# A fused attention and feed-forward kernel: later batches project q and k in plain float32 on TensorE's row halves instead of as split float32r

## The chip, the cores and the metric

The kernel runs on one core of one Trainium2 chip. The metric is the device time of the whole program in microseconds. Before the change it took 1100.27 us (median of three runs, 1098.75 to 1100.88).

## What is computed

Random-feature attention over 8 batches of 8 heads (576 tokens, 64 columns a head, 128 features), then a feed-forward layer over the 4608 tokens (512 to 2048 to 512, exact gelu). All of it is float32.

```
q_s, k_s = q * scale, k * scale            # scale = 64 ** -0.25
phi(x): proj = einsum('bhsd,md->bhsm', x, omega)
        h = proj - sum(x * x, -1) / 2
        h = h - max(h, -1)
        return exp(h) / sqrt(m)
q_p, k_p = phi(q_s), phi(k_s)
kv  = einsum('bhsm,bhsd->bhmd', k_p, v);   z = sum(k_p, axis=2)
num = einsum('bhsm,bhmd->bhsd', q_p, kv)
den = einsum('bhsm,bhm->bhs', q_p, z)[..., None] + 1e-06
x   = (num / den), heads side by side, one row a token
out = gelu(x @ w_in) @ w_out
```

Since the row maximum is taken off, the sum of squares falls out, and the kernel doesn't compute it.

## The kernel before

The attention works on units of two heads of one batch: 32 units, four a batch. The first batch (mode 0) runs before the feed-forward starts, the second (mode 1) and the other six (mode 2, 24 units) run between its matmuls. The feed-forward goes over 12 blocks of 384 tokens and, in each, over 16 chunks of 128 hidden columns. For a chunk, `mm1` (L622) makes twelve matmuls of 384 columns: each product is three, of high and low float32r parts. `act_high` and `act_low` (L629, L630, L635) make the gelu and its two parts, on ScalarE and VectorE. `mm2` (L645 to L647) adds three times three matmuls of 512 columns into three accumulators. The sets of weights are converted into high and low parts in the first fifth of the program, on ScalarE, VectorE and GpSimd (L124 to L155).

The order is written by hand. Every step is an event with a time, in units of which a chunk has 6 and a mode-2 unit 35; the events are issued in the order of their times, and the layer below may then move single instructions. What one engine is given stands in its queue in order, so an instruction that waits holds up all behind it on that engine. PSUM has three pools of banks: `at` (three buffers, all of the attention), `h` (two) and `acc` (three). A buffer of `at` is taken again when its readers are done.

In modes 0 and 1, q and k of the two heads lie on the two halves of the partitions, columns of a head on 64 rows (`x2`). `proj_pair` (L533) then makes four tiles of 128 tokens for each head, in plain float32, with the heads alternating on TensorE's upper and lower row halves. `proj_shared` (L544) makes the tile in which the end of one head meets the start of the other. `proj_mid` (L594, L596) takes the row maximum from PSUM and subtracts it into `et`, the tile of all exponents. The plain numerators (`num`, L459) use column halves.

In mode 2 both halves of the partitions hold the same q and k of both heads (two DMAs each, L223). `x_high` (L236, ScalarE) rounds a piece to float32r on all 128 rows, and `x_low` (L242, GpSimd) replaces its lower half by what the rounding lost, so that one matmul multiplies both parts. For k, five groups: `proj` (L249) multiplies by the high and low part of omega side by side, `proj_lo` (L254, ScalarE) copies the second product, `proj_add` (L260, L261, VectorE) adds it and takes the maximum, and `k_shift` (L266, GpSimd) subtracts that for all nine tiles. For q, four groups: `proj_q` (L277) makes two matmuls of 288 tokens, features on the partitions; `q_blocks` (L285, L287, VectorE) transposes blocks of 32 and takes their maxima; `q_max` (L293) to `q_max4` (L306) find the maximum of a token by two small transposes on TensorE; and `q_shift` (L312, VectorE) subtracts it. Then one exponential over `et` (`exps`, L320).

What follows is shared by both versions: k's exponents as two float16 parts (`k_high`, `k_low`), v in bfloat16 parts (`v_a` to `v_d`, GpSimd), their product in one `at` buffer (`kv`, L400), its copies (`kv_a` to `kv_d`: L409 on ScalarE, L416 to L418 on VectorE, L424, L428), and three float32r matmuls a head for the numerators (L468), whose quotients (`den`, `div`) become the rows x.

SyncE's queue issues the DMAs in order: weights, q, k, v, outputs.

Of the kernel before, what the change touches and what calls it, by code (L numbers as in the profile page):

```python
# [19 lines left out]
P = 128  # L20
# [8 lines left out]
def favor_attention_ffn(ctx: ExitStack, tc: tile.TileContext, qT, kT, v, omT, w_in, w_out, out):  # L29
# [28 lines left out]
    ident = cp.tile([P, P], F32, name="ident")  # L58
    om = cp.tile([P, 2, M], F32R, name="om")
    om32 = cp.tile([P, M], F32, name="om32")  # L60
# [3 lines left out]
    wol = cp.tile([P, NF, DM], F32R, name="wol")  # L64
    xt = cp.tile([P, 2, 2, S], F32, name="xt")
    xf = xt.rearrange("p a h s -> p (a h s)")
    x2 = xt[:, :, 0]
# [27 lines left out]
    def has(u, *ks):  # L95
        assert all(own[k] is u for k in ks), (u.b, u.j, ks)
# [108 lines left out]
    def v_ones(u):  # L205
        nc.vector.memset(u.v[:, :, D:D + 1], 1.0)
        nc.vector.memset(u.v[D:P, MID, D:D + 1], 0.0)
        nc.vector.memset(u.v[0:D, MID + 1, D:D + 1], 0.0)

    def load_x(u):  # L210
        own['x'] = u
# [5 lines left out]
        for s, src in ((1, qT), (0, kT)):  # L217
            if u.mode == 1:
                nc.sync.dma_start(x2[:, s], src[u.b, 2 * u.j:2 * u.j + 2].rearrange("h d s -> (h d) s"))
                continue  # L220
            sv = src[u.b, 2 * u.j:2 * u.j + 2].rearrange("h d s -> d h s")
            for r in range(2):
                nc.sync.dma_start(xt[r * D:(r + 1) * D, s], sv)  # L223
        nc.sync.dma_start(u.v[:, :, 0:D], v[u.b, u.j])


    XG = [(g * P, min(g + 2, NT) * P) for g in range(0, NT, 2)]
    NK = len(XG)
    XG += [(R2 + g * HS, R2 + (g + 1) * HS) for g in range(4)]
    QB = HS // 32  # L230

    def x_high(u, i):
        has(u, 'x')
        a, b = XG[i]
        u.r[i] = p2().tile([P, HS], F32R, tag="r", name="r", bufs=3)
        nc.scalar.copy(u.r[i][:, 0:b - a], xf[:, a:b])  # L236

    def x_low(u, i):
        has(u, 'x')
        a, b = XG[i]  # L240
        r = u.r[i][D:, 0:b - a]
        nc.gpsimd.tensor_tensor(r, xf[D:, a:b], r, op=ALU.subtract)  # L242

    def proj(u, i):
        ps = ps_at()
        r = u.r.pop(i)
        u.pp[i] = ps.rearrange("p (t a m) -> p t a m", t=2, a=2)
        for t in range((XG[i][1] - XG[i][0]) // P):
            nc.tensor.matmul(u.pp[i][:, t], r[:, t * P:(t + 1) * P], om, start=True, stop=True)  # L249

    def proj_lo(u, i):
        n = (XG[i][1] - XG[i][0]) // P
        u.lo[i] = p2().tile([P, 2, M], F32, tag="lo", name="lo", bufs=2)
        nc.scalar.copy(u.lo[i][:, 0:n], u.pp[i][:, 0:n, 1])  # L254

    def proj_add(u, i):
        t0, t1 = XG[i][0] // P, XG[i][1] // P
        own.update({('e', t): u for t in range(t0, t1)})
        es = et[:, t0:t1]
        nc.vector.tensor_tensor(es, u.pp.pop(i)[:, 0:t1 - t0, 0], u.lo.pop(i)[:, 0:t1 - t0], op=ALU.add)  # L260
        nc.vector.tensor_reduce(u.nm[:, t0:t1], es, axis=AX.X, op=ALU.max, negate=True)  # L261

    def k_shift(u):
        has(u, *[('e', t) for t in range(NT)])
        es = et[:, 0:NT]
        nc.gpsimd.tensor_tensor(es, es, u.nm[:, 0:NT].unsqueeze(2).broadcast_to([P, NT, M]), op=ALU.add)  # L266
        done.add((u, 'k'))

# [3 lines left out]

    def proj_q(u, g):
        ps = ps_at()
        r = u.r.pop(NK + g)
        for i in range(2):
            nc.tensor.matmul(ps[:, 0:HS], om[:, i], r, start=(i == 0), stop=(i == 1))  # L277
        u.pp[NK + g] = ps

    def q_blocks(u, g):  # L280
        own['q', g] = u
        if g == 0:
            u.mx = sp.tile([P, 4 * QB], F32, tag="mx", name="mx", bufs=1)
            u.nq = sp.tile([P, 4 * QB], F32, tag="nq", name="nq", bufs=1)
        nc.vector.transpose(ef[:, slice(*XG[NK + g])], u.pp.pop(NK + g)[:, 0:HS])  # L285
# [23 lines left out]
    def q_shift(u):  # L309
        need((u, 'nq'))  # L310
        has(u, *[('q', g) for g in range(4)])
        nc.vector.tensor_tensor(eq, eq, u.nq.unsqueeze(2).broadcast_to([P, 4 * QB, 32]), op=ALU.add)  # L312
        done.add((u, 'q'))

    def exps(u):
        if u.mode == 2:
            need((u, 'k'), (u, 'q'))
        has(u, *[('e', t) for t in range(NT)])
        has(u, *([('e', t) for t in range(NT, 2 * NT)] if u.mode == 1 else [('q', g) for g in range(4)]))
        nc.scalar.activation(et, et, AF.Exp)  # L320
        done.add((u, 'e'))

    def q_back(u, g):
        need((u, 'e'))
        has(u, ('q', g))
        u.qt[g] = p2().tile([P, HS], F32, tag="qt", name="qt", bufs=2)
        nc.vector.transpose(u.qt[g], ef[:, slice(*XG[NK + g])])  # L327

# [183 lines left out]

    def split_om():
        nc.vector.tensor_copy(om[:, 0], om32)
        nc.vector.tensor_tensor(om[:, 1], om32, om[:, 0], op=ALU.subtract)

    def load_plain(u):
        own['x'] = u
        u.nm = sp.tile([P, 2 * NT], F32, tag="nm", name="nm", bufs=2)
        for s, src in ((0, kT), (1, qT)):  # L520
            nc.sync.dma_start(x2[:, s], src[u.b, 2 * u.j:2 * u.j + 2].rearrange("h d s -> (h d) s"))
# [6 lines left out]
    def proj_pair(s, c0, c1, psf):  # L528
        pss = [psf(), psf()]
        for c in range(c0, c1):  # L530
            for hh, x0 in ((0, c * P), (1, (c + 1) * P - S % P)):
                r = slice(hh * D, (hh + 1) * D)
                nc.tensor.matmul(pss[hh][:, (c - c0) * P:(c - c0 + 1) * P], x2[r, s, x0:x0 + P], om32[r],  # L533
                                 start=True, stop=True)
        return [(ps[:, 0:(c1 - c0) * P].rearrange("p (t m) -> p t m", m=M), s * NT + t)
                for ps, t in ((pss[0], c0), (pss[1], MID + 1 + c0))]

    def proj_shared(psf):
        ps = psf()
        w = S % P  # L540
        for s in range(2):
            for hh, x0 in ((0, MID * P), (1, 0)):
                r = slice(hh * D, (hh + 1) * D)
                nc.tensor.matmul(ps[r, s * P:(s + 1) * P], x2[r, s, x0:x0 + w], om32[r], start=True, stop=True)  # L544
        return ps[:, 0:2 * P].rearrange("p (t m) -> p t m", m=M)

    def proj_parts(u, i, psf):

        has(u, 'x')
        if i == 1:  # L550
            return [(proj_shared(psf), slice(MID, MID + NT + 1, NT))]
        return [(pv, slice(t, t + MID)) for pv, t in proj_pair(i // 2, 0, MID, psf)]

# [116 lines left out]
    at(BASE - 3, make_identity, nc, ident)  # L670
    at(BASE + 5, split_om)
    for i, u in enumerate(units[:NJ]):
# [21 lines left out]
    for k, u in enumerate(units[NJ:]):  # L694
# [13 lines left out]
        else:  # L708
            pk, pq = [t - 27 + 1.75 * i for i in range(NK)], [t - 16 + 2 * i for i in range(4)]
            load_at = pq[-1] - 1.8  # L710
            for i, tt in enumerate(pk + pq):
                at(tt - 3, x_high, u, i)
                at(tt - 2.4, x_low, u, i)
                if i < NK:
                    at(tt, proj, u, i)
                    at(tt + 0.5, proj_lo, u, i)
                    at(tt + 1, proj_add, u, i)
                else:
                    at(tt, proj_q, u, i - NK)
                    at(tt + 0.4, q_blocks, u, i - NK)  # L720
            at(pk[-1] + 1.5, k_shift, u)
            for d, f in ((1.5, q_max), (2, q_max2), (2.5, q_max3), (3, q_max4), (3.5, q_shift)):
                at(pq[-1] + d, f, u)
            for d, f in enumerate((v_a, v_b, v_c, v_d)):
# [90 lines left out]
```

## Time and profile before

| | |
|---|---|
| median of three runs | 1100.27 us |
| the profiled execution, its own time | 1100.79 us |
| its span in the trace | 1098.9 us |
| granted TensorE clock, mean | 0.992 |
| HBM read, written | 60.36 MB, 9.44 MB |
| q and k loads (L219, L223, L521), each tensor | x56, 288 KB in the mean, some 3.9 us to landing |

The page slices the span into 40 parts of 27 us each and writes the busy share of an engine in tenths; nearly all slices of TensorE stand at 9 from the sixth on. "Busy" is the union of the instructions' spans, and matmul ends are modelled. Rows of groups give the line, the engine, the operation with its tiles, the count, the busy time, the mean duration of one, and the idle time of that engine just before them with what ended it. A line of the timeline gives start, duration, engine, line and operation, and merges neighbours that read alike into one row with a count.

### The profile page before, as it was taken

What the parts mean: (1) busy time and instruction counts of PE and PEld (TensorE: products, weight loads), DVE (VectorE), ACT (ScalarE), POOL (GpSimd) and SP (SyncE); (2) the same over time, 40 slices, a digit from 0 to 9 for tenths busy, and PEclk for the clock granted to TensorE, in tenths of its full rate; (3) what the DMA queues carried; (4) which work ended last, traced back from release to release, by engine and by line L of the source; (5) the groups of instructions that cost most, each with busy time, mean ns of one, the idle gap of its engine ahead of it and who ended that gap; (6) DMA issues with size and microseconds to landing.
All of it is one profiled execution on the core that took longest, in us unless ns stands there. A gap on an engine that the chain in (4) does not pass through costs nothing.

```text
span 1098.9 us, 17294 instructions
## 1 busy us (share of the span) xinstructions
PE 1049.1 (95%) x6022; PEld 906.3 (82%) x6022; DVE 789.7 (72%) x1780; ACT 618.0 (56%) x1310; POOL 482.4 (44%) x554
## 2 busy tenths in 40 slices
PE   8897899999999999999899999999999999999998
PEld 6675678888888888888778788878888888998998
DVE  5879887778878887877888878888887877411211
ACT  7856665666556466666546666654666655322321
POOL 4624546544455565444456544445654444000000
PEclk9989999999999999999999999999999999999999
DMA  8534532211211211211212211122121110000000
GB/s 232 169 110 150 164 117 60 70 44 44 75 44 56 84 56 52 62 50 47 72 56 56 75 32 56 57 62 55 56 74 41 49 63 1 1 29 1 30 1 30
DMA packets 46279, 70.92 MB, mean 65 GB/s; under 512 B 13680, under 2 KB 22256, under 8 KB 46192
## 3 DMA queue, kind: packets, MB, share of 16 engines
q1 hardware_dynamic: 46192, 69.81, 21.2%
q8 instruction: 48, 0.79, 0.3%
q14 instruction: 39, 0.32, 0.1%
HBM read 60.36 MB, written 9.44 MB: 64 GB/s over the span
## 4 chain that ended last, share of the span: by engine, by line
PE 64%; DVE 18%; ACT 2%; issue 2%; POOL 1%; POOLq 0%; ACTq 0%; DVEq 0%
PE h L622 27%; PE acc L647 9%; PE acc L646 9%; PE acc L645 9%; PE at L468 3%; PE at L400 3%; DVE gl L635 2%; DVE et L285 2%; PE at L249 2%; DVE mx L287 2%; PE at L277 1%; DVE xs L497 1%; DVE rt L485 1%; DVE rc L486 1%; DVE rt L488 1%
## 5 line engine op out<-in xcount | busy, mean ns | idle before, releaser
L622 PE MATMUL h<-xh,wih 128*128 128x384 f32 x768 | 263.2, 343 | 0.0
L622 PE MATMUL h<-xl,wih 128*128 128x384 f32 x768 | 262.5, 342 | 0.0
L622 PE MATMUL h<-xh,wil 128*128 128x384 f32 x768 | 262.0, 341 | 0.0
L645 PE MATMUL acc<-woh,gh 128*128 128x512 f32 (+1 forms) x576 | 230.8, 401 | 0.0
L647 PE MATMUL acc<-wol,gh 128*128 128x512 f32 (+1 forms) x576 | 226.6, 393 | 0.0
L646 PE MATMUL acc<-woh,gl 128*128 128x512 f32 (+1 forms) x576 | 226.2, 393 | 0.0
L635 DVE TENSOR_TENSOR gl<-g,gh 128x384 fp32r<-128x384 f32 x192 | 128.6, 670 | 121.1 <-ACT gh L630 120.6
L242 POOL TENSOR_TENSOR r<-xt,r 64x256 fp32r<-64x256 f32 (+2 forms) x216 | 173.8, 813 | 59.5 <-ACT r L236 46.4
L629 ACT ACTIVATE g<-h 128x384 f32<-128x384 f32 x192 | 94.4, 491 | 170.0 <-PE h L622 161.0
L373 POOL TENSOR_SCALAR kh<-et 128x256 f16<-128x256 f32 (+1 forms) x120 | 50.2, 425 | 280.8 <-ACT et L320 176.0
L622 PEld LDWEIGHTS h<-xh,wih 128*128 128x128 f32 x768 | 145.1, 189 | 7.7 <-issue 1.8
L622 PEld LDWEIGHTS h<-xh,wil 128*128 128x128 f32 x768 | 145.0, 189 | 6.3 <-issue 0.9
L622 PEld LDWEIGHTS h<-xl,wih 128*128 128x128 f32 x768 | 145.3, 189 | 1.3 <-issue 0.9
L647 PEld LDWEIGHTS acc<-wol,gh 128*128 128x128 f32 x576 | 108.3, 188 | 23.9
L645 PEld LDWEIGHTS acc<-woh,gh 128*128 128x128 f32 x576 | 108.5, 188 | 14.6 <-issue 1.5
L646 PEld LDWEIGHTS acc<-woh,gl 128*128 128x128 f32 x576 | 108.6, 189 | 12.8 <-issue 0.4
L236 ACT CAST r<-xt 128x256 fp32r<-128x256 f32 (+2 forms) x216 | 88.2, 410 | 51.9 <-PE at L277 44.2
L630 ACT CAST gh<-g 128x384 fp32r<-128x384 f32 x192 | 98.8, 515 | 3.3
L381 DVE SCALAR_TENSOR_TENSOR kl<-et,kh 128x256 f16<-128x256 f32 (+1 forms) x120 | 65.2, 559 | 30.7 <-POOL kh L373 28.9
L327 DVE STREAM_TRANSPOSE qt<-et 128x288 f32<-128x288 f32 x96 | 45.2, 471 | 51.8 <-ACT et L320 51.4
L141 POOL TENSOR_TENSOR wb<-wb,raw 128x512 int32<-128x512 int32 x32 | 44.0, 1376 | 67.5 <-DVE wb L137 30.3
L254 ACT COPY lo<-at 128x256 f32<-128x256 f32 (+1 forms) x120 | 41.9, 349 | 55.4 <-PE at L249 53.5
(151 smaller groups left out, 1850.2 us busy)
## 6 DMA issues: line engine op xcount, KB each, us to landing
xt<-in_kT SPq DMA_DIRECT2D x56, 288.0 KB, 3.9
xt<-in_qT SPq DMA_DIRECT2D x56, 288.0 KB, 3.8
v<-in_v SPq DMA_DIRECT2D x32, 320.0 KB, 3.1
out_x<-o SPq DMA_DIRECT2D x35, 256.0 KB, 2.1
raw<-in_w_in SPq DMA_DIRECT2D x16, 512.0 KB, 3.9
raw<-in_w_out SPq DMA_DIRECT2D x16, 512.0 KB, 3.6
out_x<-o SPq DMA_DIRECT2D x2, 128.0 KB, 1.7
om<-in_omT SPq DMA_DIRECT2D x2, 32.0 KB, 2.1
```

The source lines that it names most:

```text
L236: nc.scalar.copy(u.r[i][:, 0:b - a], xf[:, a:b])
L242: nc.gpsimd.tensor_tensor(r, xf[D:, a:b], r, op=ALU.subtract)
L327: nc.vector.transpose(u.qt[g], ef[:, slice(*XG[NK + g])])
L373: nc.gpsimd.tensor_scalar(kh[:, :n], es, KSC, 1.0, op0=ALU.mult, op1=ALU.mult)
L381: nc.vector.scalar_tensor_tensor(kl[:, :n], es, KSC, kh[:, :n], op0=ALU.mult, op1=ALU.subtract)
L622: nc.tensor.matmul(h[:, 0:T], w, (xh, xh, xl)[k], start=(i == 0), stop=(i == 3 * NJ - 1))
L629: nc.scalar.activation(g, h[:, 0:T], AF.Gelu)
L630: nc.scalar.copy(gh, g)
L635: nc.vector.tensor_tensor(gl, g, gh, op=ALU.subtract)
L645: nc.tensor.matmul(acc, gh[:, s], woh[:, c, c0:c1], start=(c == 0), stop=False)
L646: nc.tensor.matmul(acc, gl[:, s], woh[:, c, c0:c1], start=False, stop=False)
L647: nc.tensor.matmul(acc, gh[:, s], wol[:, c, c0:c1], start=False, stop=(c == NF - 1))
```

## The change

Mode 2 projects as mode 1 did. q and k of a unit are loaded once, two heads on the two halves of the partitions, into a tile `xt` that now has two buffers (`load_qk`, for all modes). For k, `proj_mid(u, 0)` makes the eight full tiles on row halves and takes the maximum and shifts, both on VectorE from PSUM; `proj_mid(u, 1)` makes the shared tile of k alone, 14.5 time units later. For q, `proj_q(u, half)` makes one plain float32 matmul of 288 tokens for each head, on its row half, into two `at` buffers; `q_blocks` then runs per head. `q_shift` moves from VectorE to GpSimd. `x_high`, `x_low`, `proj`, `proj_lo`, `proj_add`, `k_shift` and the split of omega (`split_om`) are gone. The first numerators come half a time unit later.

```diff
+    def load_qk(u):
+        own['x', u.b * NJ + u.j] = u
+        u.x = sp.tile([P, 2, S], F32, tag="xt", name="xt", bufs=2)
+        for s, src in ((0, kT), (1, qT)):
+            nc.sync.dma_start(u.x[:, s], src[u.b, 2 * u.j:2 * u.j + 2].rearrange("h d s -> (h d) s"))
...
-    def x_high(u, i):
-        nc.scalar.copy(u.r[i][:, 0:b - a], xf[:, a:b])
-    def x_low(u, i):
-        nc.gpsimd.tensor_tensor(r, xf[D:, a:b], r, op=ALU.subtract)
-    def proj(u, i):
-            nc.tensor.matmul(u.pp[i][:, t], r[:, t * P:(t + 1) * P], om, start=True, stop=True)
-    def proj_lo(u, i):
-    def proj_add(u, i):
-    def k_shift(u):
...
-    def proj_q(u, g):
-        ps = ps_at()
-        r = u.r.pop(NK + g)
-        for i in range(2):
-            nc.tensor.matmul(ps[:, 0:HS], om[:, i], r, start=(i == 0), stop=(i == 1))
+    def proj_q(u, half):
+        pss = [ps_at(), ps_at()]
+        for hh, ps in enumerate(pss):
+            r = slice(hh * D, (hh + 1) * D)
+            nc.tensor.matmul(ps[:, 0:HS], om32[r], u.x[r, 1, half * HS:(half + 1) * HS], start=True, stop=True)
+            u.pp[2 * hh + half] = ps
...
-        nc.vector.tensor_tensor(eq, eq, u.nq.unsqueeze(2).broadcast_to([P, 4 * QB, 32]), op=ALU.add)
+        nc.gpsimd.tensor_tensor(eq, eq, u.nq.unsqueeze(2).broadcast_to([P, 4 * QB, 32]), op=ALU.add)
...
-            pk, pq = [t - 27 + 1.75 * i for i in range(NK)], [t - 16 + 2 * i for i in range(4)]
-            load_at = pq[-1] - 1.8
...
+            at(t - 22.5, proj_mid, u, 0)
+            for half in range(2):
+                at(t - 20 + 3 * half, proj_q, u, half)
+                for hh in range(2):
+                    at(t - 19.6 + 3 * half + 0.1 * hh, q_blocks, u, 2 * hh + half)
+            for d, f in ((1, q_max), (1.5, q_max2), (2, q_max3), (2.5, q_max4), (3, q_shift)):
+                at(t - 16 + d, f, u)
+            at(t - 8, proj_mid, u, 1)
+            load_at = t - 7.8
...
-            tt = t + (17 + 4 * half if u.mode == 1 else 18 + 5 * half)
+            tt = t + (17 + 4 * half if u.mode == 1 else 18.5 + 5 * half)
```

What the order of the instructions shows. In TensorE's queue before, in the middle of the program, a q group is two adjacent matmuls (L277) between feed-forward matmuls (L645 to L647 the second layer, L622 the first):

```order
L645 MATMUL acc<-woh,gh 128x512
L646 MATMUL acc<-woh,gl 128x512
L647 MATMUL acc<-wol,gh 128x512
L277 MATMUL at<-r,om 128x288 x2
L622 MATMUL h<-xh,wih 128x384
```

In TensorE's queue of the changed kernel, a mode-2 unit has k's block of eight matmuls (L486, one row with x8) and eight first-layer matmuls; then, here, come the two heads of q's first half (L233) and, further on, those of its second half; L574 is the first layer now, L597 to L599 the second:

```order
L233 MATMUL at<-xt,om_65 128x288
L597 MATMUL acc<-woh,gh 128x512
L233 MATMUL at<-xt,om_65 128x288
L598 MATMUL acc<-woh,gl 128x512
L599 MATMUL acc<-wol,gh 128x512
L597 MATMUL acc<-woh,gh 128x512
L598 MATMUL acc<-woh,gl 128x512
L599 MATMUL acc<-wol,gh 128x512
L597 MATMUL acc<-woh,gh 128x512
L598 MATMUL acc<-woh,gl 128x512
L599 MATMUL acc<-wol,gh 128x512
L233 MATMUL at<-xt,om_65 128x288 x2
```

The heads of the first half are parted by one feed-forward matmul; those of the second are neighbours. This is so in all 24 units (where the one between is sometimes of the first layer).

On VectorE before, the additions and maxima of k's groups (L260, L261) stand between the kv copies (L416 to L428):

```order
L260 TENSOR_TENSOR et<-at,lo 128x256
L416 TENSOR_TENSOR kvs<-kvs 128x2x64
L261 TENSOR_REDUCE nm<-et 128x2
L417 TENSOR_TENSOR kvz<-at,kvs 128x2x64
L418 COPY kvz<-kvs 128x128
L260 TENSOR_TENSOR et<-at,lo 128x256
L261 TENSOR_REDUCE nm<-et 128x2
L428 TENSOR_TENSOR kvl<-kvz,kvh 128x256
```

On VectorE in the changed kernel, the same copies (L375 to L387) come first, then a gelu residual (L587), both maxima of k's block (L546) and both shifts (L548), then q's transposes and maxima (L244, L246):

```order
L375 TENSOR_TENSOR kvs<-kvs 128x2x64
L377 COPY kvz<-kvs 128x128
L376 TENSOR_TENSOR kvz<-at,kvs 128x2x64
L387 TENSOR_TENSOR kvl<-kvz,kvh 128x256
L587 TENSOR_TENSOR gl<-g,gh 128x384
L546 TENSOR_REDUCE nm<-at 128x4 x2
L548 TENSOR_TENSOR et<-at,nm 128x512 x2
L244 STREAM_TRANSPOSE et<-at 128x288 x2
L246 TENSOR_REDUCE mx<-et 128x9 x2
```

The two maxima stand ahead of the two shifts, and a shift is the last reader of k's PSUM buffers.

More of the change, by code (lines that the diff above doesn't have):

```diff
@@ L216, in load_x @@
         u.nm = sp.tile([P, 2 * NT], F32, tag="nm", name="nm", bufs=2)
[L217 to L223, printed above, removed]
+        load_qk(u)
         nc.sync.dma_start(u.v[:, :, 0:D], v[u.b, u.j])
-    XG = [(g * P, min(g + 2, NT) * P) for g in range(0, NT, 2)]
@@ L251, in proj_lo @@
-    def proj_lo(u, i):
-        n = (XG[i][1] - XG[i][0]) // P
-        u.lo[i] = p2().tile([P, 2, M], F32, tag="lo", name="lo", bufs=2)
-        nc.scalar.copy(u.lo[i][:, 0:n], u.pp[i][:, 0:n, 1])
-    def proj_add(u, i):
[L257 to L261, printed above, removed]
@@ L280, in q_blocks, with qcols @@
+    def qcols(g):
+        return slice(R2 + g * HS, R2 + (g + 1) * HS)
     def q_blocks(u, g):
         own['q', g] = u
-        if g == 0:
+        if not hasattr(u, 'mx'):
             u.mx = sp.tile([P, 4 * QB], F32, tag="mx", name="mx", bufs=1)
             u.nq = sp.tile([P, 4 * QB], F32, tag="nq", name="nq", bufs=1)
-        nc.vector.transpose(ef[:, slice(*XG[NK + g])], u.pp.pop(NK + g)[:, 0:HS])
+        nc.vector.transpose(ef[:, qcols(g)], u.pp.pop(g)[:, 0:HS])
         s = slice(g * QB, (g + 1) * QB)
@@ L316, in exps @@
         if u.mode == 2:
-            need((u, 'k'), (u, 'q'))
+            need((u, 'q'))
         has(u, *[('e', t) for t in range(NT)])
@@ L511, in load_om @@
         nc.vector.tensor_scalar(om32, om32, XSCALE, None, op0=ALU.mult)
-    def split_om():
-        nc.vector.tensor_copy(om[:, 0], om32)
-        nc.vector.tensor_tensor(om[:, 1], om32, om[:, 0], op=ALU.subtract)
     def load_plain(u):
-        own['x'] = u
+        load_qk(u)
         u.nm = sp.tile([P, 2 * NT], F32, tag="nm", name="nm", bufs=2)
-        for s, src in ((0, kT), (1, qT)):
-            nc.sync.dma_start(x2[:, s], src[u.b, 2 * u.j:2 * u.j + 2].rearrange("h d s -> (h d) s"))
         u.v = ep[0].tile([P, NV, D + 1], F32, tag="v1", name="v1", bufs=2)
@@ L524, in load_plain, with proj_pair, proj_shared @@
         nc.sync.dma_start(u.v[:, :, 0:D], v[u.b, u.j])
-    def proj_pair(s, c0, c1, psf):
+    def proj_pair(u, s, psf):
         pss = [psf(), psf()]
-        for c in range(c0, c1):
+        for c in range(MID):
             for hh, x0 in ((0, c * P), (1, (c + 1) * P - S % P)):
                 r = slice(hh * D, (hh + 1) * D)
[L533 to L538, printed above, removed]
+                nc.tensor.matmul(pss[hh][:, c * P:(c + 1) * P], u.x[r, s, x0:x0 + P], om32[r], start=True, stop=True)
+        return [(ps.rearrange("p (t m) -> p t m", m=M), slice(t, t + MID))
+                for ps, t in ((pss[0], s * NT), (pss[1], s * NT + MID + 1))]
+    def proj_shared(u, ss, psf):
         ps = psf()
         w = S % P
-        for s in range(2):
+        for x, s in enumerate(ss):
             for hh, x0 in ((0, MID * P), (1, 0)):
                 r = slice(hh * D, (hh + 1) * D)
-                nc.tensor.matmul(ps[r, s * P:(s + 1) * P], x2[r, s, x0:x0 + w], om32[r], start=True, stop=True)
-        return ps[:, 0:2 * P].rearrange("p (t m) -> p t m", m=M)
+                nc.tensor.matmul(ps[r, x * P:(x + 1) * P], u.x[r, s, x0:x0 + w], om32[r], start=True, stop=True)
+        return [(ps[:, 0:len(ss) * P].rearrange("p (t m) -> p t m", m=M),
+                 slice(ss[0] * NT + MID, ss[-1] * NT + MID + 1, NT))]
     def proj_parts(u, i, psf):
-        has(u, 'x')
         if i == 1:
-            return [(proj_shared(psf), slice(MID, MID + NT + 1, NT))]
-        return [(pv, slice(t, t + MID)) for pv, t in proj_pair(i // 2, 0, MID, psf)]
+            return proj_shared(u, (0, 1) if u.mode < 2 else (0,), psf)
+        return proj_pair(u, i // 2, psf)
     def proj_plain(u, i):
```

38 lines of the change are left out of this document (1 added, 37 removed).

## The prediction

> **What bounds the kernel now.** I read the page first, then the busy time by stage, then TensorE's groups and waits, then single rows of the timeline for prices.
>
> ```profile
> span 1098.9 us, 17294 instructions
> PE 1049.1 (95%) x6022; PEld 906.3 (82%) x6022; DVE 789.7 (72%) x1780; ACT 618.0 (56%) x1310; POOL 482.4 (44%) x554
> PE 64%; DVE 18%; ACT 2%; issue 2%; POOL 1%; POOLq 0%; ACTq 0%; DVEq 0%
> ```
>
> TensorE is busy for 1049.1 of 1098.9 us, and the chain that ended last runs through it for 64%. VectorE carries 18% of that chain. GpSimd, from which the change takes most, carries 1%, and ScalarE 2%.
>
> ```profile
> 0.00:200.00 200.00, 175.95 (x1138) 139.28 (x1139) 154.88 (x333) 130.24 (x273) 98.21 (x93) 0.96 0.47 141
> 200.00:920.00 720.00, 697.31 (x3944) 607.43 (x3944) 587.75 (x1354) 435.39 (x936) 381.41 (x455) 1.00 0.19 56
> ```
>
> These are the busy times by stage (TensorE, its weight loads, VectorE, ScalarE, GpSimd, then clock and DMA). The changed units, 24 of 32, lie almost all in 200 to 920 us. There TensorE idles for 720 − 697.3 = 22.7 us, or 1.0 us for each of the 23 units in that window, at a granted clock of 1.00. So in this stage time put onto TensorE is paid nearly in full, and time taken off another engine can win back at most those 22.7 us, and a little refilling after each stop. The 24 us idle in the first 200 us belong to code whose arithmetic the change leaves alone.
>
> **TensorE: the sum.** What the old projections cost:
>
> ```profile
> L249 PE MATMUL at<-om,r 128*128 128x256 f32 x216 | 47.0, 290 | 2.2 <-DVE et L260 2.2
> L277 PE MATMUL at<-r,om 128*128 128x288 f32 x192 | 42.4, 302 | 5.1 <-DVE et L285 2.8 <-DVE rc L486 1.3 <-DVE rc L487 0.8
> ```
>
> Each unit has 216/24 = 9 matmuls for k and 192/24 = 8 for q. Their mean durations (290, 302 ns) overlap their neighbours', so the price is taken from starts: how far a block puts off the feed-forward matmul behind it.
>
> ```profile
> 301.18 0.39 PE L647 MATMUL acc<-wol,gh 128*128 128x512 f32 x1
> 301.42 0.40 PE L249 MATMUL at<-om,r 128*128 128x256 f32 x2
> 301.65 0.39 PE L645 MATMUL acc<-woh,gh 128*128 128x512 f32 x1
> ...
> 306.52 0.39 PE L647 MATMUL acc<-wol,gh 128*128 128x512 f32 x1
> 306.76 0.44 PE L277 MATMUL at<-r,om 128*128 128x288 f32 x2
> 307.03 0.40 PE L645 MATMUL acc<-woh,gh 128*128 128x512 f32 x1
> ```
>
> A second-layer matmul takes 0.23 us from its start to the next one's. Two k matmuls therefore cost 301.65 − 301.18 − 0.23 = 0.24 us, two q matmuls 307.03 − 306.52 − 0.23 = 0.28 us. Nine and eight of them: 1.08 + 1.12 = **2.20 us** a unit.
>
> The new form already runs in the earlier batches, between feed-forward matmuls too. Every plain float32 matmul leaves two records in the trace, so x16 are eight.
>
> ```profile
> 142.03 0.40 PE L647 MATMUL acc<-wol,gh 128*128 128x512 f32 x1
> 142.35 0.65 PE L544 MATMUL at<-om,xt 64*64 64x128 f32 x8
> 142.94 0.45 PE L622 MATMUL h<-xh,wih 128*128 128x384 f32 x1
> ...
> 143.57 0.34 PE L622 MATMUL h<-xh,wih 128*128 128x384 f32 x1
> 143.84 1.16 PE L533 MATMUL at<-om,xt 64*128 64x128 f32 x16
> 144.93 0.44 PE L622 MATMUL h<-xh,wil 128*128 128x384 f32 x1
> ```
>
> The block of eight (four tiles for each head) costs 144.93 − 143.57 less the 0.17 us of the first-layer matmul ahead: 1.19 us. Before it stand 0.27 us instead of 0.17: entering row halves costs 0.1 us. The shared tiles of q and k, x8, cost 0.91 − 0.23 = 0.68 us.
>
> One matmul alone, with the other head's not beside it:
>
> ```profile
> 66.11 0.34 PE L622 MATMUL h<-xh,wil 128*128 128x384 f32 x1
> 66.38 0.49 PE L533 MATMUL at<-om,xt 64*128 64x128 f32 x2
> 66.80 0.44 PE L622 MATMUL h<-xl,wih 128*128 128x384 f32 x1
> ...
> 151.48 0.34 PE L622 MATMUL h<-xh,wih 128*128 128x384 f32 x1
> 151.75 0.71 PE L459 MATMUL at<-qh,kvz 128*64 128x288 f32 x4
> 152.38 0.45 PE L622 MATMUL h<-xh,wil 128*128 128x384 f32 x1
> ```
>
> Alone it costs 0.69 − 0.17 = 0.52 us. It has two passes and the block of eight has eight double ones, so a pass of 128 columns is (1.19 − 0.52)/6 = 0.112 us and the fixed part of any visit 0.52 − 0.22 = 0.30 us. For 288 columns a pass is 0.25 us and a visit with two passes 0.80 us, whether one head runs or both side by side. The plain numerators, 288 columns on column halves, cost 0.73 us by the last three rows, which is near.
>
> By the order, k's block stays whole in all 24 units, and q's second half keeps its two heads together. **In q's first half a feed-forward matmul stands between the two heads in all 24 units**, so these pay twice. The shared tile of k comes alone, half of the x8: 0.68 − 2·0.112 = 0.46 us. After: 1.19 + 0.46 + 3·0.80 = 4.05 us. That is 1.85 us more than before, and 24 units make **+44 us**.
>
> The Trainium skill, TensorEngine Tiling (Array Packing), section Key Properties, says that changing the tiling mode drains TensorE and gives no figure; this speaks against the change, and the 0.27 us ahead of the L533 block agrees. TensorE: Matmul & The Clock Gate, in the Trainium skill, section Measured speedup vs the span model, prices packed tiles at one matmul plus about 4 ns for each further tile; by that rule alone, with no fixed part, an estimate would make the sum some 24·5·0.30 = 36 us smaller, and the rows above speak against it.
>
> Bounds. Below: if the split heads ran as cheaply as one pair at L459's price, q would cost 1.46 and the sum would be +21 us (shared tile 0.44). Above: if a lone matmul grew in full proportion to its columns, 0.52·288/128 = 1.17 each, +62 us. I take 44, since two independent rows (0.73 and the 0.80 worked out) meet there.
>
> **The other engines.** What goes, and what comes:
>
> ```profile
> L242 POOL TENSOR_TENSOR r<-xt,r 64x256 fp32r<-64x256 f32 (+2 forms) x216 | 173.8, 813 | 59.5 <-ACT r L236 46.4 <-PE h L622 2.0 <-PE at L249 1.5
> L236 ACT CAST r<-xt 128x256 fp32r<-128x256 f32 (+2 forms) x216 | 88.2, 410 | 51.9 <-PE at L277 44.2 <-POOL r L242 4.0 <-POOL wb L141 1.5
> L254 ACT COPY lo<-at 128x256 f32<-128x256 f32 (+1 forms) x120 | 41.9, 349 | 55.4 <-PE at L249 53.5
> L260 DVE TENSOR_TENSOR et<-at,lo 128x256 f32<-128x256 f32 (+1 forms) x120 | 46.3, 386 | 3.1 <-ACT lo L254 2.9
> L261 DVE TENSOR_REDUCE nm<-et 128x2 f32<-128x256 f32 (+1 forms) x120 | 46.1, 384 | 2.0
> L312 DVE TENSOR_TENSOR et<-et,nq 128x1152 f32<-128x1152 f32 x24 | 32.6, 1357 | 8.2 <-ACT nq L306 7.7
> L266 POOL TENSOR_TENSOR et<-et,nm 128x1152 f32<-128x1152 f32 x24 | 51.6, 2151 | 2.1 <-DVE nm L261 0.6
> L594 DVE TENSOR_REDUCE nm<-at 128x4 f32<-128x512 f32 x16 | 10.4, 679 | 3.3 <-PE at L533 3.2
> ```
>
> GpSimd loses L242's 173.8 us; k's shift (51.6) goes and q's shift of the same shape takes its place. ScalarE loses 88.2 + 41.9 = 130 us. VectorE loses 46.3 + 46.1 + 32.6 = 125 us and gains, in each unit, two reductions and two shifts of 128x512 at 0.68 (a shift costs as much as a reduction here) and one small pair at 0.28: 3.3 us, 79 us in all, so 46 us net go. None of this is on TensorE, and I count it as nothing but for waits. The shift of q is placed 13 of the 35 time units of a head pair ahead of the exponential, some 11 us here, so its 2.15 us are covered by the feed-forward matmuls there; without that cover it would cost (2.15 − 1.36)·24 = 19 us. The DMAs of q and k halve in a stage where DMA is at 0.19.
>
> **Waits.** The old projections' own waits go: 2.2 + 5.1 = 7 us by L249 and L277, some 9 with refilling. New is this. The first k block takes two of the three PSUM buffers, kv has the third, and the second head of q's first half needs the first of them back. Its release now stands on VectorE behind the kv copies:
>
> ```profile
> L409 ACT COPY kvs<-at 128x258 f32<-128x258 f32 x24 | 9.1, 381 | 3.7 <-PE at L400 3.7
> L416 DVE TENSOR_TENSOR kvs<-kvs 128x128 f32<-128x128 f32 x24 | 13.1, 545 | 1.6 <-ACT kvs L409 1.6
> L418 DVE COPY kvz<-kvs 128x128 f32<-128x128 f32 x24 | 17.3, 722 | 0.0
> L428 DVE TENSOR_TENSOR kvl<-kvz,kvh 128x256 fp32r<-128x256 f32 x24 | 13.4, 558 | 0.5 <-ACT kvh L424 0.5
> ```
>
> From kv's last matmul these four take 2.2 us, then two reductions and one shift 2.0: 4.2 us. TensorE meanwhile has four matmuls (0.7), the block (1.19), eight matmuls (1.4), the first head (0.80) and one matmul (0.23): 4.3 us. So the wait is about 0 at best; with a gelu residual (0.67) and the copies I left out between, up to 1.3 us, 31 us in all. Behind the waiting instruction the whole feed-forward stands. I take 0.4 us, 10 us in all, which cancels the 9 that go. For the first 200 us I take 0: there only the second buffer for q and k is new, and what SyncE's queue loses in waits I can't place on the chain (ends: −10 us and +3).
>
> The profiled execution took 1100.8 us, 0.5 above the median of the runs shown. 1100.8 + 44 + 10 − 9 = 1146, rounded down a little for a less loaded VectorE: **1145 us**.
>
> **Rivals.**
> 1. *Less is paid.* TensorE's added work falls where it would have stood still, and freer engines end the rest of the 22.7 us (24 for 24 units): 1100.8 + 44 − 24 = 1121. Or a visit to row halves has no fixed part in this stage: five visits less 0.30 us in 24 units, 44 − 36 = 8 and 1109. For the first speaks that VectorE is relieved by 46 us; against it that q's and kv's waits hang on VectorE's chain behind the same matmuls; against the second, the 0.27 us ahead of L533. 18%, most of it the first. The page with the span model, cited above, is the second.
> 2. *VectorE's queue becomes the wait.* The upper 1.3 us at the second head come in every unit: 1145 + 24·0.9 = 1167, up to 1180. For it: both k reductions stand ahead of both releasing shifts. Against: GpSimd disturbs VectorE less. 14%.
> 3. *Faster: VectorE's chain sets the pace.* Then its loss of 46 us, and the end of GpSimd's 173.8 us beside it, take away every stop of the span (1098.9 − 1049.1 = 49.8 us), and the time falls to TensorE's own work: 1049.1 + 44 + 1.9 outside the span = 1095 us. It decides where the relief exceeds the added 44 us.
>
> ```profile
> L635 DVE TENSOR_TENSOR gl<-g,gh 128x384 fp32r<-128x384 f32 x192 | 128.6, 670 | 121.1 <-ACT gh L630 120.6
> ...
> L635 DVE TENSOR_TENSOR gl<-g,gh 128x384 fp32r<-128x384 f32 x19 | 10.6, 557 | 60.5 <-ACT gh L630 60.5
> ```
>
> The second row is the same work in 1000 to 1080 us, where GpSimd does nothing: 557 ns against 670. So VectorE does suffer from GpSimd, 22 us on this line. Against the rival: 88% of the stops would have to go, and half of them lie in the first 200 us. 8%. The Trainium skill, SBUF — State Buffer, section SBUF: two separate sides, says that a VectorE operation with two SBUF inputs and a GpSimd operation hold one port pair against each other, whole instructions long; the two means agree.
>
> **How the numbers follow.** The forecast, TensorE's work paid and the waits about even, gets 60% (1128 to 1163). Rival 1 has 18%, rival 2 14%, rival 3 8%. A range from 1110 to 1172 leaves out rival 3 and the far ends of the others, under 2 in 10. A measurement of this kernel can tell about 0.2% from no change; faster by more than that 7% (nearly all of rival 3), within it 2%, slower 91%.
>
> **What would show it.** In the changed kernel's trace: two records of q for each head, the first head's pair with a feed-forward matmul behind it, each putting the next one off by 0.8 us; k's block still at 1.19; TensorE busy near 1093 us; VectorE near 740 or less, GpSimd near 310; TensorE's waits on k's shift (the new L548) some 10 us. The forecast is wrong if a lone q matmul costs 0.5 instead of 0.8, or if TensorE's idle time in the stage moves by more than 20 us either way.

## The result and the profile after

The changed kernel took 1142.41 us (median of four runs, 1141.95 to 1143.03), the kernel before on the same chip 1100.58 us: a ratio of 1.0384, 95% interval [1.0366, 1.0402], or 41.8 us more. The profiled execution took 1143.03 us. First the page of the changed kernel: span, busy times, chain.

```profile
span 1141.2 us, 16733 instructions
PE 1103.7 (97%) x6286; PEld 900.0 (79%) x6286; DVE 714.2 (63%) x1658; ACT 513.4 (45%) x974; POOL 308.1 (27%) x338
PE 81%; DVE 9%; ACT 2%; issue 1%; POOL 0%; DVEq 0%; ACTq 0%; POOLq 0%
```

VectorE has lost 75 us, ScalarE 105, GpSimd 174, and the span has grown by 42.3 us, because TensorE is busy for 54.6 us more. Busy times by stage, columns as before:

```profile
0.00:200.00 200.00, 178.41 (x1149) 138.10 (x1150) 154.12 (x331) 127.71 (x261) 88.95 (x82) 0.96 0.46 138
200.00:960.00 760.00, 747.11 (x4184) 600.25 (x4183) 513.46 (x1231) 332.01 (x610) 216.31 (x251) 0.99 0.11 35
540.00:550.00 10.00, 7.33 (x22) 4.86 (x20) 6.08 (x10) 1.09 (x3) 1.75 (x2) 0.67 0.12 33
910.00:920.00 10.00, 7.57 (x22) 5.20 (x23) 6.17 (x14) 1.00 (x2) 0.21 (x1) 0.66 0.10 33
950.00:960.00 10.00, 10.00 (x47) 8.53 (x48) 5.83 (x18) 2.04 (x6) 2.13 (x1) 0.85 0.00 0
```

The first stage moved little: the same feed-forward matmul starts at 191.56 us before and at 191.90 now, 0.3 us later. Counted by the same matmuls, the changed kernel is then 4 us behind at 300 us, 18 at 500, 28 at 800 and 42 at 920; it falls behind most slowly between 500 and 800 us, where the kernel before had most of its own stops. TensorE's idle time in the stage fell from 22.7 to 12.9 us. But the granted clock, 1.00 there before, drops in three places (the last three rows). TensorE's waits (line, releaser: sum in us, times, longest) hold only one of any size after 200 us:

```profile
PE at L233 <- DVE et L548: 12.3, 11, 2.7
```

That is the forecast wait: the second head of q's first half, on k's shift. The prices, from the timeline:

```profile
305.26 0.39 PE L599 MATMUL acc<-wol,gh 128*128 128x512 f32 x1
305.57 1.16 PE L486 MATMUL at<-om,xt 64*128 64x128 f32 x16
306.67 0.50 PE L597 MATMUL acc<-woh,gh 128*128 128x512 f32 x1
307.00 0.39 PE L598 MATMUL acc<-woh,gl 128*128 128x512 f32 x1
...
307.98 0.34 PE L574 MATMUL h<-xh,wih 128*128 128x384 f32 x1
308.25 0.75 PE L233 MATMUL at<-xt,om 64*128 64x288 f32 x2
308.93 0.44 PE L574 MATMUL h<-xh,wil 128*128 128x384 f32 x1
...
312.14 0.40 PE L599 MATMUL acc<-wol,gh 128*128 128x512 f32 x1
312.47 0.76 PE L233 MATMUL at<-xt,om 64*128 64x288 f32 x4
313.15 0.50 PE L597 MATMUL acc<-woh,gh 128*128 128x512 f32 x1
313.49 0.39 PE L598 MATMUL acc<-woh,gl 128*128 128x512 f32 x1
```

k's block puts the next matmul off by 306.67 − 305.26 − 0.23 = 1.18 us, one head of q by 308.93 − 307.98 − 0.17 = 0.78, two adjacent heads by 313.15 − 312.14 − 0.23 = 0.78: one head costs what two do. The matmul after the next is late as well: 306.67 to 307.00 and 313.15 to 313.49 are 0.33 and 0.34 us instead of 0.23. **Leaving row halves costs another 0.1 us**, which the prediction's price rows ended too early to see.

Why the waits are long shows in the timeline of VectorE and GpSimd ahead of the longest one:

```profile
537.00 0.72 POOL L302 TENSOR_SCALAR vb<-v 128x640 bf16<-128x640 f32 x1 [1.49 <-PE at L359]
537.81 1.53 POOL L308 TENSOR_TENSOR v<-v,vb 128x640 f32<-128x640 f32 x1
538.05 1.45 DVE L375 TENSOR_TENSOR kvs<-kvs 128x128 f32<-128x128 f32 x1
...
540.30 1.54 POOL L320 TENSOR_TENSOR vb<-v,vb 128x640 bf16<-128x640 f32 x1
540.54 1.58 DVE L387 TENSOR_TENSOR kvl<-kvz,kvh 128x256 fp32r<-128x256 f32 x1
542.04 1.28 DVE L546 TENSOR_REDUCE nm<-at 128x4 f32<-128x512 f32 x2
543.24 1.27 DVE L548 TENSOR_TENSOR et<-at,nm 128x512 f32<-128x512 f32 x2
...
544.07 0.81 PE L233 MATMUL at<-xt,om 64*128 64x288 f32 x1 [2.67 <-DVE et L548]
```

GpSimd, freed of `x_low`, stands idle until kv (L359) has read the old v and splits the new one at once, just where VectorE copies kv. Here each kv copy ends 0.2 to 0.3 us after GpSimd's subtraction (539.50 after 539.34, 542.12 after 541.84), and k's maxima and shifts stand behind them. The copies are this long in two of the 24 units only, those of the waits of 2.67 and 2.50 us. In the six units with waits of about 1 us it is above all the gelu residual (L587) among the same operations that is held by v's split: at 339.16 us it takes 1.45 us instead of 0.55, and the wait behind it is 1.04 us.

### The profile page after: what moved, and what is told of

Its sections match the earlier page's. It is cut to its first block, busy times and chain, and to the rows that moved or that the text cites. A ratio compares the mean times of both kernels' runs of the same rounds, so it can differ in the third digit from the quotient of the medians.

```text
span 1141.2 us, 16733 instructions
## 1 busy us (share of the span) xinstructions
PE 1103.7 (97%) x6286; PEld 900.0 (79%) x6286; DVE 714.2 (63%) x1658; ACT 513.4 (45%) x974; POOL 308.1 (27%) x338
## 4 chain that ended last, share of the span: by engine, by line
PE 81%; DVE 9%; ACT 2%; issue 1%; POOL 0%; DVEq 0%; ACTq 0%; POOLq 0%
PE h L574 35%; PE acc L597 11%; PE acc L598 11%; PE acc L599 11%; PE at L233 4%; PE at L427 3%; PE at L359 3%; DVE nm L546 2%; DVE gl L587 1%; PE at L486 1%; DVE et L548 1%; DVE wb L133 1%; DVE kvl L387 1%; PE at L496 1%; DVE wol L151 1%
## 5 line engine op out<-in xcount | busy, mean ns | idle before, releaser
L574 PE MATMUL h<-xh,wih 128*128 128x384 f32 x768 | 267.5, 348 | 0.7 <-ACT xh L557 0.6
L574 PE MATMUL h<-xl,wih 128*128 128x384 f32 x768 | 267.1, 348 | 0.0
L574 PE MATMUL h<-xh,wil 128*128 128x384 f32 x768 | 267.0, 348 | 0.0
L597 PE MATMUL acc<-woh,gh 128*128 128x512 f32 (+1 forms) x576 | 239.0, 415 | 0.0
L599 PE MATMUL acc<-wol,gh 128*128 128x512 f32 (+1 forms) x576 | 226.9, 394 | 0.0
L587 DVE TENSOR_TENSOR gl<-g,gh 128x384 fp32r<-128x384 f32 x192 | 122.1, 636 | 153.5 <-ACT gh L582 151.4
L574 PEld LDWEIGHTS h<-xh,wih 128*128 128x128 f32 x768 | 146.5, 191 | 14.6 <-issue 6.4
L574 PEld LDWEIGHTS h<-xh,wil 128*128 128x128 f32 x768 | 146.6, 191 | 14.0 <-issue 7.4
L574 PEld LDWEIGHTS h<-xl,wih 128*128 128x128 f32 x768 | 146.9, 191 | 7.9 <-issue 6.1
L597 PEld LDWEIGHTS acc<-woh,gh 128*128 128x128 f32 x576 | 108.8, 189 | 29.5 <-issue 13.9
L599 PEld LDWEIGHTS acc<-wol,gh 128*128 128x128 f32 x576 | 108.6, 188 | 24.0
L271 POOL TENSOR_TENSOR et<-et,nq 128x1152 f32<-128x1152 f32 x24 | 52.6, 2192 | 207.3 <-ACT nq L265 207.3
L340 DVE SCALAR_TENSOR_TENSOR kl<-et,kh 128x256 f16<-128x256 f32 (+1 forms) x120 | 50.7, 434 | 36.0 <-POOL kh L332 35.6
L233 PE MATMUL at<-xt,om 64*128 64x288 f32 x192 | 55.7, 470 | 12.6 <-DVE et L548 12.3
L279 ACT ACTIVATE et<-et 128x2304 f32<-128x2304 f32 x28 | 59.7, 2131 | 0.3
L244 DVE STREAM_TRANSPOSE et<-at 128x288 f32<-128x288 f32 x96 | 41.3, 465 | 26.0 <-PE at L233 26.0
```

The source lines that it names most:

```text
L233: nc.tensor.matmul(ps[:, 0:HS], om32[r], u.x[r, 1, half * HS:(half + 1) * HS], start=True, stop=True)
L271: nc.gpsimd.tensor_tensor(eq, eq, u.nq.unsqueeze(2).broadcast_to([P, 4 * QB, 32]), op=ALU.add)
L340: nc.vector.scalar_tensor_tensor(kl[:, :n], es, KSC, kh[:, :n], op0=ALU.mult, op1=ALU.subtract)
L574: nc.tensor.matmul(h[:, 0:T], w, (xh, xh, xl)[k], start=(i == 0), stop=(i == 3 * NJ - 1))
L587: nc.vector.tensor_tensor(gl, g, gh, op=ALU.subtract)
L597: nc.tensor.matmul(acc, gh[:, s], woh[:, c, c0:c1], start=(c == 0), stop=False)
```

## The experiments

"Late v" below means a GpSimd operation on one column ahead of v's split, reading a maximum, so that the split can't start earlier; the split overwrites it. Medians are of four runs where no other number is given; each ratio is to the kernel before on the same chip. There the kernel before took 1098.1 to 1098.8 us beside the experiments and 1100.6 beside the changed kernel, so a difference between times from different chips is good to some 2 us.

**1. The waits taken away (hold_v).** v's split waits for k's maxima.

```diff
     def v_a(u):
+        nc.gpsimd.tensor_scalar(vb[:, 0, 0:1], u.nm[:, 0:1], 1.0, 1.0, op0=ALU.mult, op1=ALU.mult)
         nc.gpsimd.tensor_scalar(vb[:, :, 0:D], u.v, 1.0, 1.0, op0=ALU.mult, op1=ALU.mult)
```

> The changed kernel with one 128x1 operation on GpSimd ahead of v's split, which reads k's maxima, so that the split cannot run beside the kv copies on VectorE. If GpSimd's split is what makes those copies long (means of 580 ns for the first and 837 ns for the residual, with up to 1445 and 1578), they fall to about 300 and 450 ns, the waits for k's shift from 12 us to under 4, and the half-clock stretches after the longest waits go: 1122 to 1133. Rival, the order of VectorE's queue alone makes the wait: within 4 us of 1142.

1121.21 us (1120.88 to 1122.64), 1.0204 [1.0189, 1.022], just below the range. The two copies in VectorE's groups, then a window of 740 us:

```profile
L376 DVE TENSOR_TENSOR kvs<-kvs 128x128 f32<-128x128 f32 x24 | 7.0, 293 | 27.1 <-ACT kvs L369 27.1
L388 DVE TENSOR_TENSOR kvl<-kvz,kvh 128x256 fp32r<-128x256 f32 x24 | 10.2, 425 | 9.4 <-ACT kvh L384 9.4
200.00:940.00 740.00, 739.62 (x4188) 595.50 (x4187) 500.20 (x1231) 332.66 (x611) 215.47 (x273) 1.00 0.11 36
```

The copies fall from means of 580 and 837 ns to 293 and 425. TensorE idles for 0.4 of 740 us and the clock is 1.00 throughout. So waits and what follows them cost the changed kernel 1142.4 − 1121.2 = **21.2 us**, and TensorE's work alone, less all stops of before, is worth +22.

**2. q's two heads adjacent (pairs).** k's block is issued earlier; q's first half then runs as a pair in all 24 units.

```diff
-            at(t - 22.5, proj_mid, u, 0)
+            at(t - 24.5, proj_mid, u, 0)
```

> k's block two time units earlier, after which the two heads of q's first half stand side by side in all 24 units. If the sum of the prediction holds (every visit to the row halves has its fixed price), one visit of some 0.85 us goes in each unit, 20 us, and the 12 us of waits for k's shift go with it, since k's buffers come free before q's first half: 1142 becomes 1100 to 1115, waits for k's shift under 3 us. Rival, the added time is the passes of plain float32 themselves and not the visits: no less than 1125.

1112.13 us (1111.25 to 1112.87), 1.0119 [1.0104, 1.0134]: 30.3 us less than the changed kernel. Its timeline:

```profile
305.41 0.34 PE L574 MATMUL h<-xh,wih 128*128 128x384 f32 x1
305.68 0.76 PE L233 MATMUL at<-xt,om 64*128 64x288 f32 x4
306.37 0.45 PE L574 MATMUL h<-xh,wil 128*128 128x384 f32 x1
...
308.34 0.40 PE L599 MATMUL acc<-wol,gh 128*128 128x512 f32 x1
308.67 1.01 PE L233 MATMUL at<-xt,om 64*128 64x288 f32 x4
309.61 0.50 PE L597 MATMUL acc<-woh,gh 128*128 128x512 f32 x1
```

The first pair takes 306.37 − 305.68 = 0.69 us, the second 0.94: a wait inside the merged row (both take 0.69 in experiment 3). The kv copies are longer still here (means 1127 and 1470 ns). **With both edits (pairs_hold_v):**

> Both edits. If both act on the same wait, the time is that of the pairs alone within 4 us (1100 to 1115); if they add up, some 10 us below the pairs.

1115.5 us (1115.17 to 1115.58), 1.0149 [1.0132, 1.0166]: nothing adds up, and the time is 3.4 us above that of the pairs. With k's block this early its maxima stand ahead of the kv copies in VectorE's order; the hold parts nothing and the copies stay at 1215 and 1470 ns.

**3. The split held longer (pairs_late_v).** As pairs, with v's split behind q's maxima (`u.mx` in place of `u.nm`).

> The pairs, and v's split held until q's maxima, which there come after the kv copies (holding until k's maxima did not part them in that order). The two copies fall from 1127 and 1470 ns to about 300 and 430, and a wait inside the second pair of q heads (0.94 us against 0.69 for the first) goes: 9 us less than the pairs, about 1103. Rival, VectorE's queue makes that wait: within 3 us of 1112.

1110.45 us (1110.16 to 1111.03), 1.0107 [1.009, 1.0124]. The copies fell to 283 and 422 ns and both pairs to 0.69, but only 1.7 us came of it where 9 were expected: the rival's number, though the wait that it spoke of is gone. TensorE's waits name the new stop:

```profile
PE at L262 <- DVE sm L258: 10.6, 19, 1.6
PE at L428 <- DVE et L244: 1.2, 2, 0.6
```

The small transpose of q's maxima now comes 19 times before VectorE has it ready.

**4. One visit less (merged).** As pairs_late_v, and k's shared tile directly behind q's second half, in the same PSUM buffer.

```diff
     def proj_q(u, half):
+        if half:
+            u.sh = proj_shared(u, (0,), lambda: pss[0], HS)
...
-            at(t - 8, proj_mid, u, 1)
+            at(t - 15.5, proj_mid, u, 1)
```

> The run before this one, and k's shared tile put behind q's second half in the same PSUM buffer, so that it is no visit of its own. If entering and leaving the row halves is what a visit costs beside its passes, 0.57 becomes about 0.25 to 0.35 a unit, 5 to 8 us less than pairs_late_v: 1096 to 1098, level with the kernel before. Rival, the column halves of the shared tile are a mode of their own and pay the entry all the same: no gain over pairs_late_v.

1099.91 us (ten runs, 1097.85 to 1101.39), 1.0009 [0.9999, 1.0018]: level with the kernel before, and 10.5 us less than the run before this one, where 5 to 8 were expected. Pair and shared tile cost 1.25 us together, 0.89 + 0.57 apart (means over the units, to the second matmul behind), so 0.2 us a unit, 5 us, is the saved entry and exit; the rest of the 10.5 us is the waits, which fall from 11.8 to 4.1 us (the two together would make 12.7):

```profile
PE at L254 <- DVE et L551: 2.6, 6, 0.6
PE at L430 <- DVE et L246: 1.0, 3, 0.3
PE at L264 <- DVE sm L260: 0.5, 2, 0.3
```

**5. The change for k alone (k_alone)**, q left in float32r: the kernel before with `proj_mid` for k, at t − 24.5 and t − 12, in place of `x_high` to `k_shift` for k's groups.

> The kernel before with only k in plain float32 on row halves (q stays split in float32r). By the prices read in the changed kernel, 1.29 for the block with its exit and 0.57 for the shared tile against 1.08 before, TensorE gets 0.78 us a unit, 19 us; VectorE is rid of the additions, which may take up to 8 us of waits: 1112 to 1120. Rival, k costs nothing and q is all of the loss: 1101 within 3 us.

1111.77 us (1111.02 to 1113.19), 1.0117 [1.0101, 1.0134], at the lower end of the range. The stops of before are here joined into one:

```profile
PE at L471 <- DVE kvl L431: 14.7, 22, 1.0
PE at L471 <- ACT kvh L427: 1.7, 1, 1.7
```

The numerators wait for the kv copies (928 and 1305 ns), held by v's split again. **With the late v (k_alone_late_v):**

> k in plain float32 alone, with v's split held until q's maxima. Its waits of 14.7 and 1.7 us for the last kv copy and its rounding go if GpSimd's split makes the copies long (1305 ns in the mean): 1095 to 1100, level with the kernel before although TensorE has 19 us more to do. Rival, they stay: 1108 or more.

1104.26 us (1103.13 to 1104.55), 1.0049 [1.0034, 1.0064], again less gained than I expected (1095 to 1100): the copies are at 282 and 424 ns and that wait is gone, but the next of VectorE's chain ends late.

```profile
PE at L280 <- DVE et L288: 9.3, 15, 0.9
```

**6. q's shift on GpSimd, alone.** In the kernel before (before_shift), and undone in hold_v (hold_shift_dve): one word, `nc.vector` or `nc.gpsimd`, in `q_shift`.

> The kernel before with one edit of the change alone: q's shift on GpSimd instead of VectorE. If the stops of the kernel before come from VectorE being full, its 33 us less take some of the 22 us away: 1093 to 1097. If they come from where GpSimd's work lies beside VectorE's, 52 us more on GpSimd leave or lengthen them: 1098 to 1104.

> hold_v (1121.2 us) with q's shift back on VectorE. The prediction costs this part of the change at nothing: covered by feed-forward matmuls on either engine, so 1120 to 1123 us and no new wait. Rival: VectorE's 1.36 us a unit lie on the path (the relief of VectorE is what keeps the changed kernel at its time): TensorE's waits on VectorE rise by 10 to 30 us, 1131 to 1150 us. Other side: GpSimd's 2.15 us shift holds VectorE's operations with two SBUF inputs, and taking it away wins: 1115 to 1119 us.

1097.28 us (ten runs), 0.9985 [0.997, 1.0], and 1121.34 us (1120.8 to 1121.98) beside hold_v's 1121.21. A relief of VectorE by 32 us is worth 0 to 3 us before, at the border of the two forecasts, and nothing after. TensorE's idle time between 200 and 920 us falls from 22.7 to 19.5 us: the wait of L468 for `kvl` goes from 4.6 to 0.5, but the largest that are left were there before as well, and have grown (from 3.4 and 4.5):

```profile
PE at L468 <- DVE xs L496: 5.1, 5, 1.5
PE at L293 <- DVE mx L287: 4.9, 13, 0.5
```

**7. Longer waits, by VectorE alone (waits_graded):** hold_v with k's first maximum repeated one to six times in one unit of each later batch.

```diff
+            for _ in range(u.b if u.mode == 2 and u.j == 1 and i == 0 and ts.start == 0 else 1):
                 nc.vector.tensor_reduce(u.nm[:, ts], pv, axis=AX.X, op=ALU.max, negate=True)
```

> hold_v (1121.2 us, no wait of TensorE between 200 and 940 us) with k's maximum over its first four tiles taken more than once in one unit of each later batch: 2, 3, 4, 5, 6 and 7 times in batches 2 to 7, so 1 to 6 reductions of 0.68 us more ahead of the releasing shift, 21 in all. Up to some 0.5 us of each are hidden; the six waits at the second head of q's first half should be about 0.2, 0.9, 1.5, 2.2, 2.9 and 3.6 us, 11 us in all. Theory 1 (a long wait itself brings the half clock): the granted clock falls to 0.5 for some 6.8 us behind the waits above 2.5 us, perhaps for 3.4 us behind those of 1 to 2.2 us, and at no other place; each costs half its length: 1121.2 + 11 + about 10 = 1142 us. Theory 2 (the half clock of the changed kernel fell there by another cause, the waits only beside it): 1.00 behind all six, 1132 us.

1125.46 us (1125.08 to 1125.87), 1.025 [1.0235, 1.0265]. Both forecasts are missed, and it doesn't decide the clock: the layer below moved TensorE's instructions, so that hardly a wait arose (0.5 us in all). In four units it parted q's second pair; 4.3 us for four more visits is again about one microsecond each. Beside that, the 14 us more on VectorE left nothing to be seen.

**8. Longer waits, with TensorE's order kept (port_stall):** the changed kernel; in 12 units GpSimd repeats its last subtraction of v's split once or twice, and VectorE repeats 32 columns of the `kvl` subtraction as often.

```diff
     def v_d(u):
+        for _ in range(1 + (u.j + 1) // 2 * (u.j % 2)):
             nc.gpsimd.tensor_tensor(vb[:, :, 2 * D + 1:VW], u.v, vb[:, :, D:2 * D], op=ALU.subtract)
...
         nc.vector.tensor_tensor(u.kvl, u.kvz, u.kvh, op=ALU.subtract)
+        for _ in range((u.j + 2) // 2 * (1 - u.j % 2)):
+            nc.vector.tensor_tensor(u.kvl[:, 0, 0:32], u.kvz[:, 0, 0:32], u.kvh[:, 0, 0:32], op=ALU.subtract)
```

> The changed kernel (1142.4 us) in which, in 12 of the 24 units, GpSimd repeats the last subtraction of v's split (1.54 us, two SBUF inputs) once (6 units) or twice (6 units), and VectorE repeats as often 32 columns of the kvl subtraction right behind it, ahead of k's maxima; TensorE's order is that of the changed kernel. Theory 1 on VectorE: an operation with two SBUF inputs stands until GpSimd's running operation ends, so each small one, under 0.15 us by itself, shows up to 1.5 us, and the wait at the second head of q's first half grows by up to 1.5 or 3 us. Rival: the small operations show under 0.2 us, no wait grows, 1143 us. Theory 1 on the clock: waits above 2.5 us are each followed by the granted clock 0.5 for some 6.8 us. With the first and without the second: 1142 + 6 x (1 to 1.5) + 6 x (2 to 3) = 1160 to 1169 us; with both, 6 to 12 waits at 3.4 us more each: 1180 to 1210 us.

1154.5 us, 1.0494 [1.0447, 1.0541]; two runs at 1149.8, two at 1159.2 and 1159.65 (the profiled one), all below both forecasts. The timeline, the waits, and windows with the clock:

```profile
547.90 4.47 POOL L321 TENSOR_TENSOR vb<-v,vb 128x640 bf16<-128x640 f32 x3
548.15 1.58 DVE L388 TENSOR_TENSOR kvl<-kvz,kvh 128x256 fp32r<-128x256 f32 x1
549.76 1.22 DVE L390 TENSOR_TENSOR kvl<-kvz,kvh 128x32 fp32r<-128x32 f32 x1
...
552.93 0.82 PE L233 MATMUL at<-xt,om 64*128 64x288 f32 x1 [3.93 <-DVE et L551]
553.30 0.17 DVE L390 TENSOR_TENSOR kvl<-kvz,kvh 128x32 fp32r<-128x32 f32 x1
...
PE at L233 <- DVE et L551: 23.5, 19, 3.9
...
340.00:350.00 10.00, 7.69 (x36) 5.26 (x35) 8.10 (x14) 1.36 (x4) 5.81 (x5) 0.81 0.11 33
550.00:560.00 10.00, 7.07 (x25) 5.43 (x26) 6.34 (x14) 1.00 (x2) 2.29 (x2) 0.66 0.12 33
930.00:940.00 10.00, 10.00 (x45) 8.24 (x46) 5.99 (x19) 2.58 (x7) 2.03 (x1) 0.84 0.01 2
```

The same 32 columns take 0.17 us with GpSimd idle and 1.22 us beside its subtractions, ending at 550.98, as the second of the three does (547.90 + 2 · 1.49 = 550.88). Waits rose from 12.3 to 23.5 us, less than I gave: 14 of the 18 small operations took 0.6 us or less. The half clock rose with them, from 17 us in all to 34, in seven stretches instead of three. The 11.2 us of waits more, and 8.5 for 17 us more at half speed, make 19.7, where the profiled execution took 16.6 us more.

## Why the prediction was right, and where its terms were not

**The total** (1145) was 2.6 us above the result, and the forecast's case, TensorE's added work, is what happened. That it came so close is luck: the added work was 10 us larger than forecast, the old waits that go 22 us larger, and the new wait and a term that was left out add 10 us.

- **Work of the projections, +44.** The entry prices held: k's block 1.18 (1.19 forecast), shared tile 0.46 (0.46), one head 0.78 and a pair 0.78 (0.80 each). Missing was the exit, 0.1 us on the second matmul behind each of five visits, 12 us over 24 units. By the means over hold_v's units (an estimate from starts, good to some 3 us, as the next one is), visits now cost some 54 us more than before. The split of q's first half, which the order showed, holds a whole visit: 30 us came back with pairs, some 22 to 24 of it from the visit (0.9 to 1.0 us in 24 units), the rest from waits and clock, less the new waits of the pairs.
- **The old waits, −9.** Too small. I let only L249's and L277's go; in hold_v all 22.7 us are gone, those of the numerators (L468) and of q's maxima (L293) too. Summed over the visits, with the slow restart behind each, the stops of before come to some 31 us. That makes 54 − 31 = +23, and hold_v measured +22. The experiments don't settle which edit freed which wait (q's projection was not changed alone): the move of q's shift alone freed little, and the change of k alone moved them to L471 and L280.
- **The new wait, +10.** Its place, its releaser and its size (12.3 us) were right. Its cause was only half given: not the copies' own length, but GpSimd's v split holding them and the gelu residual; hold_v, which parts them, has no such wait. The GpSimd work taken away, which I counted for nothing but less disturbance, came back as a collision. That GpSimd is early because `x_low` is gone is read from its idle time ahead of the split (1.49 us above); no run put that work back.
- **Not in the sum:** the half clock behind the longest waits, 8.5 us (17 us at half speed).
- Together: 54 − 31 + 12 + 8.5 = 44 against 41.8 measured. The rest, 2 us, I can't place.
- **q's shift at nothing:** right, 1121.34 against 1121.21. **The first 200 us at nothing:** right within 1 us.
- **Rivals.** The first, *less is paid*, was at work with its 22.7 us of stops that go, but the exits, the new waits and the clock took them back. The second's queue did hold up TensorE, 11 times instead of 24. The third falls: VectorE lost 75 us, more than the 46 counted, since unchanged operations became shorter too (the copy into `kvz` from 722 to 215 ns in the mean, `kl` from 559 to 434), and TensorE's work still set the time. The forecast's two tests (a lone q matmul at 0.5; idle time moved by more than 20 us) did not fire: 0.78, and 22.7 to 12.9. Of the other signs, TensorE was busy for 1103.7 us instead of some 1093, by the exits and the slow clock; GpSimd's 308 us and k's block were as forecast.

No version here beats the kernel before beyond doubt. The new form, with heads adjacent, shared tile merged and v late, is level with it (1.0009); the kernel before with q's shift on GpSimd has 0.9985 [0.997, 1.0].

## What to carry to other kernels

Price a change of TensorE's tiling by visits, not by matmuls: here entry and exit cost 0.2 us, one head as much as two, so work for row halves belongs together and neighbours in the order can be worth more than relief of other engines (here 22 to 24 us, against 0 to 3 for 32 us less on VectorE). When an engine is freed, look for what it will now do earlier and whom that meets: here a free GpSimd ran into the very VectorE chain that TensorE waits for. A wait that is gone uncovers the next one of the same chain, so test removals in combination.

## What the runs showed of the hardware

- **VectorE beside GpSimd.** In these traces a kv copy or the 32-column operation, both with two SBUF inputs, that starts inside one of the subtractions of GpSimd's v split ends up to 0.3 us after it, the gelu residual 0.4 us: 0.29 us became 1.45, 0.42 became 1.58, and 32 columns went from 0.17 to 1.22. The Trainium skill, SBUF — State Buffer, section SBUF: two separate sides, calls the shared port pair an exclusive lock held for a whole instruction; the traces agree.
- **The clock after a wait.** After 200 us, every wait above 2.2 us in these two kernels (2.67 and 2.50 in the changed one; 3.93, 2.50, 2.30 and twice 2.31 in port_stall) had a granted clock of 0.5 begin in it or within 1.7 us of its end, for 3.4 or 6.8 us. In the first 200 us it isn't so: a wait of 2.45 us at 133 us in the changed kernel, and one of 2.42 at 134 in port_stall, left the clock at 1.00. Of the waits between 0.85 and 1.05 us after 200 us some brought it (0.91 at 276 us in port_stall, 1.05 at 948 in the changed kernel), others not (0.99 at 383 in port_stall, 1.04 at 342 in the changed kernel). Waits of up to 1.6 us in the kernel before brought none after 200 us. The stretches lie on a raster of their own: in the changed kernel they begin at 543.4, 912.1 and 949.6 us, which are 108 and 11 times 3.413 us apart, and the seven of port_stall are whole multiples of it apart too. The Trainium skill, TensorE: Matmul & The Clock Gate, section Part 1: The HAM clock gate (the "warmup" mystery), has the clock halved after an idle window of some 3.4 us whose phase is free. The stretches' lengths and their raster agree; waits far shorter than it were enough here, and the measurement decides. Why one wait of about 1 us brought the half clock and another did not stays open. The 10 us between the runs of port_stall go with the clock: its mean was 0.990 in the two at 1149.8 us and 0.978 and 0.979 in the two at 1159. A phase that differs from run to run would explain that; it wasn't tested.
